# A chunked retention layer with a gated MLP: q and k of half the blocks transposed by DMA, and another order of the jobs

## The chip, the cores and the metric

The kernel runs on one core of one Trainium2 chip. The core has five engines that work side by side: TensorE (PE), VectorE (DVE), ScalarE (ACT), GpSimd (POOL) and SyncE (SP). In this kernel SP issues nearly all DMA transfers, in the order in which they stand in its queue, and 16 DMA engines move them. The metric is device time in microseconds (us).

## The reference

Eight sequences of 576 tokens, eight heads of 64. The first half is a retention layer (attention without softmax, with a decay for each head), the second an MLP whose gate mixes the tokens of a sequence.

```python
scores = scale * np.matmul(q, k.transpose(0, 1, 3, 2))
gamma = 1.0 - 2.0 ** (-5.0 - np.arange(H))
Dmat = np.where(rel >= 0, gamma[:, None, None] ** rel, 0.0)      # rel = query place - key place
x = np.matmul(scores * Dmat, v)                                  # then [B, S, 512]
...
h = gelu(x @ w_in)                # 512 -> 1024
u, v = h[..., :512], h[..., 512:]
v_n = (v - mean) / sqrt(var + 1e-6) * g_ln
v_s = np.einsum('ts,bsd->btd', w_sg, v_n) + b_sg[None, :, None]
out = x + (u * v_s) @ w_out
```

Inputs and output are float32; the matmuls run in bfloat16.

## The kernel before, in words

**Tiling.** Two sequences make a pair (four pairs, 0 to 3) of 1152 tokens, 9 tiles of 128. A pair is cut into five blocks (list `RB`): two of 256 tokens, a half one of 128 (the last 64 tokens of one sequence and the first 64 of the other), and two of 256 again. Blocks are numbered 0 to 19 over all pairs, so pairs 2 and 3 are blocks 10 to 19.

**A block's jobs.**
- `a_load` (L428, L431): q, k and v from HBM to a buffer "ld" each (12 of these), 512 KB for a full block in one DMA, 256 KB for a half block in two. SP issues them.
- `a_prep` (L450, L456): POOL scales q and v by powers of gamma (vector `gqv`) and casts q, k, v to bfloat16: q and k into one tile "qkb" (2 buffers), v into "vb" (3).
- `a_T` (L496), called T below: PE transposes qkb, 32 matmuls against the identity for a full block, 16 for a half one, into a PSUM tile "pp" (2 buffers, shared with the scores and the outputs of attention). `a_Tev` (L505): DVE copies it to "qkT" (2 buffers).
- `a_S` (L528), S: scores k q^T inside the block, from qkT. `a_Sev` (L541): DVE multiplies by the causal mask into "ret".
- `a_Z` (L560), Z: PE adds k^T v to a running state in PSUM "zp"; `a_Zev` (L569): ACT copies it to "zb". This is what a block hands to later ones.
- `a_O`, `a_O2` (L581), O: PE multiplies ret by v and zb by q (again from qkT); `a_Oev` (L637): ACT writes the result, transposed, to "xT".

**The MLP's jobs**, by token tile or by half sequence: `m_V` (L648, the gate's half of w_in), `m_Vg` (ACT), `m_stats` (DVE, L663 and L664), `m_rs` (POOL, L668 to L671: four small steps), `m_norm` (ACT, L683), `m_U` (L695, the other half of w_in), `m_Ug` (ACT, L705), `m_W` (L714: the mixing matrix w_sg times the normalized tiles, five matmuls a job, called W), `m_Wg` (DVE, L724), `m_O` (L741, w_out), `m_Oev`, `m_store` (L761). From pair 1 on the residual x is brought from xT to "xr" by a DMA transpose that SP issues (`m_X`, L750), 128 x 512 elements of 2 bytes, and DVE adds it (L757).

**Fillers.** While PE would be idle early on, it runs matmuls on a tile of zeros ("scr<-warm", L338).

**What sets the order.** All jobs are put on a list with an engine, an assumed duration and their dependencies, and the string `ORDER` holds the order by job number (f9 is a filler of nine units). `Planner.follow` takes each engine's jobs in that order and works out start times with the assumed durations; `emit` calls the jobs by planned start. Each engine then executes its own jobs strictly in the order of the string. The constant `FETCH` is part of this: the planner assumes that PE's code arrives in blocks of 256 instructions and that a block takes that many ns. It changes no instruction by itself; only `ORDER` does.

Of the kernel before, what the change touches and what calls it, by code (L numbers as in the profile page):

```python
# [19 lines left out]
FETCH = 4800.0  # L20
# [5 lines left out]
    '0 f9 1 6 81 2 111 83 7 f11 84 112 3 8 85 114 86 120 89 12 f5 115 f5 113 13 116 118 117 f4 121 119 283 123 284 87 '  # L26
    '124 287 5 88 288 9 127 4 285 23 289 128 24 290 291 82 14 125 292 129 294 90 293 122 f5 126 295 286 296 130 304 '
    '132 305 301 133 308 11 17 10 134 309 25 306 80 310 297 311 135 136 312 15 302 16 298 315 32 307 137 33 313 320 '
    '316 314 131 139 22 34 303 140 327 325 328 321 299 317 330 138 329 141 300 143 142 326 331 18 322 334 19 144 332 '
    '366 20 333 37 318 21 367 336 99 335 370 100 319 35 368 323 371 145 97 373 93 98 95 94 372 91 36 96 377 324 92 '  # L30
    '146 382 337 147 26 148 27 369 374 38 149 378 156 39 387 152 388 150 153 383 338 375 154 348 40 339 355 349 151 '
    '346 344 155 347 389 376 29 157 356 390 437 345 392 353 379 44 438 340 391 354 384 342 158 30 393 31 41 341 28 '
    '163 439 343 161 385 159 162 401 386 43 350 160 394 164 440 402 396 165 395 42 360 397 45 398 441 361 47 351 166 '
    '172 442 458 46 167 443 380 403 445 381 444 103 173 363 352 104 459 446 49 404 447 170 460 405 168 48 179 171 448 '
    '364 461 451 169 449 174 53 105 452 399 450 180 106 175 400 462 176 455 479 463 51 182 464 453 181 465 107 54 454 '
    '357 108 183 188 469 358 52 480 109 470 184 110 177 456 189 185 101 472 457 365 190 178 466 50 473 102 481 467 '
    '186 56 524 468 482 474 484 483 471 406 475 421 525 407 362 476 187 485 57 412 486 422 477 528 413 487 359 191 '
    '478 61 526 529 490 527 55 416 530 408 417 531 410 197 409 491 63 532 411 192 414 533 423 415 195 424 545 193 546 '
    '206 538 194 488 539 196 199 434 489 534 535 435 198 436 428 536 67 208 537 58 540 429 431 430 541 59 542 547 432 '
    '200 504 207 548 600 550 492 62 549 425 493 512 500 426 554 543 501 201 433 601 559 555 520 551 560 427 68 202 '  # L40
    '552 602 60 203 204 603 418 205 496 419 557 553 420 64 604 558 556 544 209 497 621 561 605 210 622 498 606 502 '
    '607 215 608 503 499 70 216 623 213 624 222 211 65 214 563 614 609 611 212 615 217 562 494 616 612 223 495 610 '
    '224 625 613 218 642 626 513 628 219 618 72 617 505 514 643 627 632 506 233 619 516 220 225 687 584 226 635 688 '
    '231 633 66 629 221 636 515 637 507 630 232 631 508 638 71 510 620 509 644 511 227 634 689 645 517 647 242 228 '
    '646 651 518 648 639 73 229 649 79 521 230 652 77 690 564 641 650 691 640 565 234 522 692 708 235 694 251 592 570 '
    '693 568 69 571 566 519 653 572 596 567 569 236 573 238 585 240 654 703 586 237 709 588 695 704 241 701 239 696 '
    '249 698 697 763 699 710 78 250 702 700 243 587 764 523 711 244 582 713 260 574 712 705 583 580 575 714 581 245 '
    '765 246 247 766 593 715 706 720 594 707 716 595 717 721 576 248 589 718 75 722 719 767 590 723 724 252 768 253 '
    '597 769 276 577 770 725 784 578 254 258 256 598 774 257 675 259 771 775 76 255 785 655 726 679 777 772 656 74 '
    '773 665 778 591 261 786 262 788 787 274 599 776 805 667 263 789 806 779 790 666 579 671 781 780 663 791 672 673 '  # L50
    '664 275 782 264 792 783 674 267 800 793 795 801 659 265 796 657 660 794 661 798 266 662 658 797 807 799 277 808 '
    '278 676 802 810 809 268 677 279 803 683 269 850 811 678 280 745 812 680 851 746 668 681 813 735 755 669 852 682 '
    '816 272 853 270 273 759 804 814 670 729 736 271 871 281 872 684 815 730 282 737 854 685 873 738 686 855 747 874 '
    '856 743 857 727 744 876 731 728 858 732 756 859 817 733 757 760 734 758 739 875 861 761 860 748 751 862 866 762 '
    '749 863 818 867 740 819 868 824 741 822 825 742 869 877 830 823 828 878 838 752 879 750 880 829 753 885 881 846 '
    '870 820 886 754 864 821 882 834 865 831 835 887 826 832 836 827 833 889 839 842 837 888 847 840 883 841 848 910 '
    '890 884 896 849 891 902 894 897 892 895 843 893 911 844 845 903 912 918 900 904 913 898 901 905 906 899 922 908 '
    '907 914 909 919 923 920 921 915 924 916 925 917 '
# [22 lines left out]
class Planner:  # L81
# [50 lines left out]
    def place(self, j, t):  # L132
        j.start = t
        if j.nbytes:
            n = j.nbytes / j.run / 16.0 / j.parts
            at = t
            for part in range(j.parts):
                if part and len(self.dmas) >= 8:
                    at = max(at, self.dmas[-8])
                room, full = 160.0 - n, 0.0  # L140
                for end, m in reversed(self.ring):
                    room -= m
                    if room < 0:
                        full = end
                        break
                self.dma_free = max(self.dma_free, at + 1500.0) + (9.5 + 0.0385 * j.run) * n
                at = max(at + j.dur / j.parts, full)
                self.ring.append((self.dma_free, n))
                j.out = self.dma_free + 1500.0
                self.dmas.append(j.out)  # L150
            self.free[j.eng] = at
        else:
            late = 0.0
            if j.eng == "PE":
                while self.count + j.ins > 256 * self.block:
                    at = t + j.dur * (256 * self.block - self.count) / j.ins + late
                    late += max(0.0, self.landed - at)
                    self.landed = max(self.landed, at) + FETCH
                    self.block += 1
                self.count += j.ins  # L160
            j.out = t + j.dur + late
            self.free[j.eng] = j.out - OVL[j.eng]
        if j.port:
            self.port = j.out
        if j.mode is not None:
            self.mode = j.mode
        for b in j.new:
            self.order[b.tag].append(b)
# [65 lines left out]
def kernel(  # L234
# [31 lines left out]
    BUFS = dict(ld=12, wst=2, qkb=2, vb=3, qkT=2, ret=4, zb=4, xT=2, uT=2, vg=3, mv=3, vn=10, ob=3, xr=3,  # L266
# [15 lines left out]
    XP = 1  # L282

# [148 lines left out]

    def a_prep(b, t):
# [4 lines left out]
        if t in "qk" and (b, "qkb") not in st:  # L438
            st[b, "qkb"] = new("qkb", [128, 2, KK, 2, 2, D], BF)
        if t == "v":  # L440
            st[b, "vb"] = new("vb", [128, 2, H, D], BF)
            dst = st[b, "vb"][:, :ns].rearrange("p s h d -> p h s d")
        else:
            dst = st[b, "qkb"][:, "qk".index(t), :, :ns].rearrange("p k s c d -> p c (k s) d" if ns == 2 else "p k s c d -> p (s c) k d")
            src = src.rearrange("p (c k) s d -> p c (k s) d" if ns == 2 else "p (c k) s d -> p (s c) k d", c=2)
# [7 lines left out]
        if t == "q":  # L453
            g = g.rearrange("p (c k) s -> p c (k s)" if ns == 2 else "p (c k) s -> p (s c) k", c=2)
# [27 lines left out]
    def a_T(b):  # L482
# [3 lines left out]
        st[b, "qkT"] = new("qkT", [128, 2, 2, KK, 128], BF)  # L486
        tpf = tp[:].rearrange("p c a k s t -> p c (a k s t)")
        qkb = st[b, "qkb"]
# [13 lines left out]
    def a_Tev(b):  # L502
        ns = RB[b % NBK][0]
        w = 2 * KK * ns * 64
        ins = nc.vector.tensor_copy(st[b, "qkT"][:].rearrange("p c a k t -> p c (a k t)")[:, :, :w],  # L505
                                    st.pop((b, "tp"))[:].rearrange("p c a k s t -> p c (a k s t)")[:, :, :w])
        unfence(ins, ("T", b))

    def qkT_of(b, r, c, a, kk):
        ns = RB[b % NBK][0]  # L510
        w = ns * 64
        f_ = st[b, "qkT"][64 * r:64 * r + 64].rearrange("p c a k t -> p c (a k t)")
        return f_[:, c, (a * KK + kk) * w:(a * KK + kk + 1) * w]

    def a_S(b, g):
# [7 lines left out]
        for n, kk in enumerate(kks):  # L523
            for ks in range(ns):
                o = (n * ns + ks) * cs
                for r in range(2):
                    for c in range(2):
                        ins = nc.tensor.matmul(sc[64 * c:64 * c + 64, r, o:o + cs],  # L528
                                               qkT_of(b, r, c, 1, kk)[:, ks * 64:ks * 64 + 64], qkT_of(b, r, c, 0, kk),
# [19 lines left out]
    def a_Z(b, c, first):  # L549
# [7 lines left out]
        for kk in range(KK):  # L557
            for s in range(ns):
                for hh in range(2):
                    ins = nc.tensor.matmul(z[64 * hh:64 * hh + 64, kk, :], st[b, "qkb"][R, 1, kk, s, hh, :],  # L560
# [320 lines left out]
    for b in range(NBL):  # L881
# [12 lines left out]
        tpb = Buf("pp")  # L894
        jT = add("PE", 565.0 * h, t0, lambda b=b: a_T(b), deps=[jq, jk], new=[tpb, B_qkT[b]], uses=[B_qkb[b]], mode="Q", ins=33 * ns)
        jTe = add("DVE", 90 + 1130.0 * h, t0 + 700.0, lambda b=b: a_Tev(b), deps=[jT], uses=[tpb, B_qkT[b]])
# [165 lines left out]
```

## Time and profile before

| | |
|---|---|
| median of 13 runs | 214.26 us (213.31 to 215.47) |
| the profiled execution | 214.28 us, of which the traced span is 212.6 |
| granted TensorE clock | 0.997 of full speed |
| instructions in the span | 8117 |
| HBM read, written | 32.79 MB, 9.44 MB |
| DMA mean | 218 GB/s |

Times inside the profile count from the start of the span. Busy time is the time in which an engine had an instruction running; matmuls overlap, so a busy PE is not PE at its peak, and the distance from one start to the next says what a job of matmuls really occupies. A row of the timeline gives the start, the duration, the engine, the line in the kernel, the operation and "output<-input" by the names of the tiles; what stands in brackets is the idle time just before it and what ended that. "Issue" there means that the engine waited for nothing that the profile shows. In the 40 slices one digit is the busy share of 5.3 us in tenths. For DMA instructions on SP, "SPq", the duration is the time in which SP was held to issue the transfer; "to landing" counts from the issue to the arrival of the data.

### The profile page before, as it was taken

What the parts mean: (1) busy time and instruction counts of PE and PEld (TensorE: products, weight loads), DVE (VectorE), ACT (ScalarE), POOL (GpSimd) and SP (SyncE); (2) the same over time, 40 slices, a digit from 0 to 9 for tenths busy, and PEclk for the clock granted to TensorE, in tenths of its full rate; (3) what the DMA queues carried; (4) which work ended last, traced back from release to release, by engine and by line L of the source; (5) the groups of instructions that cost most, each with busy time, mean ns of one, the idle gap of its engine ahead of it and who ended that gap; (6) DMA issues with size and microseconds to landing.
All of it is one profiled execution on the core that took longest, in us unless ns stands there. A gap on an engine that the chain in (4) does not pass through costs nothing.

```text
span 212.6 us, 8117 instructions
## 1 busy us (share of the span) xinstructions
PE 201.0 (95%) x3514; PEld 136.0 (64%) x3514; DVE 147.4 (69%) x266; ACT 124.1 (58%) x214; POOL 113.6 (53%) x157
## 2 busy tenths in 40 slices
PE   7997699899999999999999999999999999999990
PEld 3564467677668677676776766756777676666650
DVE  6678647379756786615886786977947994757662
ACT  3359589937786768556667566664583336454100
POOL 5352777894769945970499759807398010202000
PEclk9999999999999999999999999999999999999998
DMA  6999999999999999799998899937960262555575
GB/s 167 290 339 255 277 252 312 276 332 291 211 259 320 291 311 272 206 272 267 239 312 155 177 265 229 194 119 181 225 140 2 78 151 77 148 148 149 152 208 163
DMA packets 84742, 46.29 MB, mean 218 GB/s; under 512 B 28826, under 2 KB 77986, under 8 KB 84706
## 3 DMA queue, kind: packets, MB, share of 16 engines
q1 hardware_dynamic: 84688, 45.77, 86.3%
q8 instruction: 27, 0.44, 0.9%
q14 instruction: 9, 0.07, 0.2%
q10 hardware_dynamic: 18, 0.00, 0.0%
HBM read 32.79 MB, written 9.44 MB: 199 GB/s over the span
## 4 chain that ended last, share of the span: by engine, by line
PE 85%; DMA 5%; ACT 3%; issue 2%; DVE 1%; POOL 1%; SPq 1%; DVEq 0%
PE wp L714 18%; PE op L741 14%; PE hu L695 13%; PE hv L648 13%; PE pp L581 7%; PE scr L338 5%; PE pp L496 5%; PE pp L528 4%; DMA wst<-in_moe_w_sg_dram 4%; PE zp L560 3%; PE wtp L822 1%; DMA xr<-xT 1%; PE op L736 1%; ACT xT L637 1%; ACT L655 1%
## 5 line engine op out<-in xcount | busy, mean ns | idle before, releaser
L456 POOL TENSOR_TENSOR qkb<-ld,gqv 128x1024 bf16<-128x1024 f32 (+1 forms) x19 | 32.7, 1722 | 20.6 <-DMA ld<-in_q_dram 7.1
L541 DVE TENSOR_TENSOR ret<-pp,msk 128x1024 bf16<-128x1024 f32 x32 | 38.1, 1214 | 7.1 <-PE pp L528 5.6
L714 PE MATMUL wp<-wT,vn 128*128 128x288 bf16 x256 | 40.6, 286 | 0.0
L724 DVE TENSOR_TENSOR uT<-wp,uT 128x288 bf16<-128x288 f32 x64 | 28.3, 451 | 17.6 <-PE wp L714 16.3
L456 POOL TENSOR_TENSOR vb<-ld,gqv 128x1024 bf16<-128x1024 f32 (+1 forms) x20 | 34.6, 1731 | 5.5 <-PE pp L581 3.8
L695 PE MATMUL hu<-xT,w_in 128*128 128x256 bf16 (+1 forms) x320 | 37.4, 262 | 0.0
L648 PE MATMUL hv<-w_in,xT 128*128 128x512 bf16 x144 | 36.7, 379 | 0.3 <-DVE w_in L368 0.3
L741 PE MATMUL op<-w_out,uT 128*128 128x512 bf16 x144 | 35.8, 380 | 0.0
L695 PEld LDWEIGHTS <-w_in 128*128 128x128 bf16 x320 | 27.9, 98 | 7.0
L637 ACT ACTIVATE xT<-pp 128x512 bf16<-128x512 f32 (+1 forms) x40 | 24.7, 670 | 11.6 <-PE pp L581 10.0
L668 POOL TENSOR_SCALAR mv<-mv 128x2 f32<-128x2 f32 (+1 forms) x20 | 4.5, 224 | 48.8 <-DVE mv L664 46.2
L714 PEld LDWEIGHTS <-vn 128*128 128x128 bf16 x256 | 24.7, 98 | 8.3
L663 DVE BATCH_NORM_STATS2 bst<-vg 128x6 f32<-128x512 f32 x36 | 24.7, 685 | 7.7 <-ACT vg L655 7.7
L655 ACT ACTIVATE vg<-hv 128x512 f32<-128x512 f32 x36 | 21.5, 596 | 13.3 <-PE hv L648 6.2
L705 ACT ACTIVATE uT<-hu 128x512 bf16<-128x512 f32 x36 | 21.3, 595 | 11.7 <-PE hu L695 11.5
L683 ACT ACTIVATE vn<-vg,mv 128x512 bf16<-128x512 f32 x32 | 25.1, 810 | 5.0 <-POOL mv L671 5.0
L505 DVE COPY qkT<-pp 128x2048 bf16<-128x2048 bf16 (+1 forms) x20 | 22.3, 1113 | 7.3 <-PE pp L496 7.1
L757 DVE TENSOR_TENSOR ob<-op,xr 128x512 f32<-128x512 f32 x27 | 18.4, 689 | 8.9 <-PE op L741 7.3
L569 ACT ACTIVATE zb<-zp 128x256 bf16<-128x256 f32 x32 | 12.2, 382 | 15.5 <-PE zp L560 15.5
L648 PEld LDWEIGHTS <-xT 128*128 128x128 bf16 x144 | 13.5, 98 | 11.9 <-ACT xT L637 0.3
L741 PEld LDWEIGHTS <-uT 128*128 128x128 bf16 x144 | 13.0, 98 | 12.3 <-DVE uT L724 0.4
L714 PE MATMUL wp<-wT,vmid 128*128 128x288 bf16 x64 | 18.3, 287 | 0.0
(79 smaller groups left out, 243.0 us busy)
## 6 DMA issues: line engine op xcount, KB each, us to landing
out_dram<-ob SPq DMA_DIRECT2D x36, 256.0 KB, 4.4
ld<-in_q_dram SPq DMA_DIRECT2D x16, 512.0 KB, 7.3
ld<-in_k_dram SPq DMA_DIRECT2D x16, 512.0 KB, 7.3
ld<-in_v_dram SPq DMA_DIRECT2D x16, 512.0 KB, 5.8
wst<-in_moe_w_in_dram SPq DMA_DIRECT2D x2, 1024.0 KB, 8.3
wst<-in_moe_w_sg_dram SPq DMA_DIRECT2D x2, 576.0 KB, 6.7
ld<-in_q_dram SPq DMA_DIRECT2D x8, 128.0 KB, 5.1
ld<-in_k_dram SPq DMA_DIRECT2D x8, 128.0 KB, 5.5
```

The lines of the kernel that those rows point to most:

```text
L456: eng.tensor_tensor(dst, src, g.unsqueeze(3).to_broadcast(list(src.shape)), op=Alu.mult)
L505: ins = nc.vector.tensor_copy(st[b, "qkT"][:].rearrange("p c a k t -> p c (a k t)")[:, :, :w], st.pop((b, "tp"))[:].rearrange("p c a k s t ...
L541: ins = nc.vector.tensor_tensor(ret[:].rearrange("p r (k t) -> p (r k) t", k=2), sc[:].rearrange("p r (k t) -> p (r k) t", k=2), msk2[:].r ...
L637: nc.scalar.activation(dst, src, Act.Copy)
L648: ins = nc.tensor.matmul(hv[:], xTs[p][:, m, kk, :], w_in[:, kk, F2:], start=(kk == 0), stop=(kk == KK - 1))
L655: unfence(nc.scalar.activation(vgs[i][:], cur.pop(("hv", i))[:], Act.Gelu_apprx_tanh), ("V", i))
L663: nc.vector.bn_stats(bst[:], vgs[i][:])
L683: nc.scalar.activation(vn[:], vg[:], Act.Identity, scale=mv[:, s, 2:3], bias=mv[:, s, 3:4])
L695: ins = nc.tensor.matmul(hu[:, n, :], w_in[:, kk, 128 * c:128 * c + 128], xTs[p][:, m:m + w, kk, :], start=(kk == 0), stop=(kk == KK - 1), ...
L714: ins = nc.tensor.matmul(ps[:], vns[t0 + j][e][:, 128 * c:128 * c + 128], wT[e][j][:, half * HS:(half + 1) * HS], start=(j == 0), stop=(j ...
L724: ins = nc.vector.tensor_tensor(uTs[p][:, c, col:col + HS], cur.pop(("wp", b, c, half))[:], uTs[p][:, c, col:col + HS], op=Alu.mult)
L741: ins = nc.tensor.matmul(op[:], uTs[p][:, c, r], w_out[:, c, :], start=(p >= XP and c == 0), stop=(c == KK - 1), skip_group_check=True)
```

## The change

For the blocks from `TB` = 10 on (pairs 2 and 3), the job on PE and the copy on DVE are replaced by one job on SP, which issues a DMA transpose straight from qkb to qkT: 128 x 2048 elements of 2 bytes for a full block (8 of them), 128 x 1024 for a half one (2). The first ten blocks keep `a_T` and `a_Tev`. In the new layout the two 64-column halves "c" of a 128-column group lie side by side after the transpose, so that S and O read q of a full block as two runs of 64 columns, 128 apart, where it was one run of 128. Half blocks now have the same order (group, half) in qkb as full ones. qkT has three buffers in place of two. `FETCH` is 7200 ns for blocks of code that the planner has arriving up to 32 us and 4800 after that (4800 throughout before), and `ORDER` is another string: on all engines jobs stand in another order, from the start on.

```diff
-FETCH = 4800.0
+FETCH = (7200.0, 4800.0)
...
-    '0 f9 1 6 81 2 111 83 7 f11 84 112 3 8 85 114 86 120 89 12 f5 115 f5 113 13 116 118 117 f4 121 119 283 123 284 87 '
+    '0 f9 1 2 82 6 111 83 7 f10 84 112 3 80 12 87 85 88 113 114 115 8 120 81 273 118 9 274 116 90 275 86 f6 119 121 '
...
-                    self.landed = max(self.landed, at) + FETCH
+                    self.landed = max(self.landed, at)
+                    self.landed += FETCH[self.landed > 32000.0]
...
-    BUFS = dict(ld=12, wst=2, qkb=2, vb=3, qkT=2, ret=4, zb=4, xT=2, uT=2, vg=3, mv=3, vn=10, ob=3, xr=3,
+    BUFS = dict(ld=12, wst=2, qkb=2, vb=3, qkT=3, ret=4, zb=4, xT=2, uT=2, vg=3, mv=3, vn=10, ob=3, xr=3,
...
+    TB = 10
...
+    def a_TX(b):
+        ns = RB[b % NBK][0]
+        st[b, "qkT"] = new("qkT", [128, 2048], BF)
+        nc.sync.dma_start_transpose(st[b, "qkT"][:, :ns * 1024].rearrange("p (g t) -> p g t", t=128),
+                                    st[b, "qkb"][:, :ns * 1024])
...
+        if b < TB:
+            return f_.rearrange("p (c a k s t) -> p c a k s t", c=2, a=2, k=KK, s=ns)[:, c, a, kk]
+        return f_.rearrange("p (a k s c t) -> p c a k s t", c=2, a=2, k=KK, s=ns)[:, c, a, kk]
...
-        tpb = Buf("pp")
-        jT = add("PE", 565.0 * h, t0, lambda b=b: a_T(b), deps=[jq, jk], new=[tpb, B_qkT[b]], uses=[B_qkb[b]], mode="Q", ins=33 * ns)
-        jTe = add("DVE", 90 + 1130.0 * h, t0 + 700.0, lambda b=b: a_Tev(b), deps=[jT], uses=[tpb, B_qkT[b]])
+        if b < TB:
+            tpb = Buf("pp")
+            jT = add("PE", 565.0 * h, t0, lambda b=b: a_T(b), deps=[jq, jk], new=[tpb, B_qkT[b]], uses=[B_qkb[b]], mode="Q", ins=33 * ns)
+            jTe = add("DVE", 90 + 1130.0 * h, t0 + 700.0, lambda b=b: a_Tev(b), deps=[jT], uses=[tpb, B_qkT[b]])
+        else:
+            jTe = add("SP", 2400.0 * ns, t0, lambda b=b: a_TX(b), deps=[jq, jk], new=[B_qkT[b]], uses=[B_qkb[b]],
+                      nbytes=262144 * ns, run=256)
```

## The prediction

> **What bounds the kernel now.** I read the summary of busy time first, then the busy slices, then the table of stretches, then PE's timeline in the one stretch that isn't full. The profiled execution took 214.28 us around a span of 212.6; the median of the runs shown is 214.26, so the sum below, made against 214.28, stands for the median too.
>
> ```profile
> PE 201.0 (95%) x3514; PEld 136.0 (64%) x3514; DVE 147.4 (69%) x266; ACT 124.1 (58%) x214; POOL 113.6 (53%) x157
> ...
> DMA  6999999999999999799998899937960262555575
> ...
> PE 85%; DMA 5%; ACT 3%; issue 2%; DVE 1%; POOL 1%; SPq 1%; DVEq 0%
> ```
>
> ```profile
> 16.90:44.90 28.00, 23.32 (x497) 16.03 (x497) 16.74 (x31) 22.91 (x41) 20.30 (x23) 1.00 1.05 278
> 44.90:90.00 45.10, 45.10 (x893) 32.57 (x886) 34.09 (x58) 31.82 (x57) 33.02 (x39) 1.00 1.05 276
> 90.00:166.00 76.00, 76.00 (x1489) 52.50 (x1488) 54.43 (x90) 47.15 (x83) 48.64 (x63) 1.00 0.91 196
> ```
>
> In the second fence the columns are the stretch, its length, the busy time of PE, weight loads, DVE, ACT and POOL, the granted clock, the DMA share and GB/s. From 44.9 us to the last matmul PE is busy without a hole: what leaves PE there shortens the run, and what any other engine saves there does not. DMA is the second resource: a share of 0.91 to 1.05 until 166, 1.13 between 60 and 80. Only the first 45 us hold idle PE time.
>
> **Part 1: the transposes leave PE.** The job T of one full block is 32 matmuls on one line:
>
> ```profile
> 103.18 0.64 PE L496 MATMUL pp<-ident,qkb 64*128 64x64 bf16 x32
> 103.75 0.44 PE L560 MATMUL zp<-vb,qkb 64*64 64x64 bf16 x16
> ```
>
> From the start of T to the start of the next job is 103.75 - 103.18 = 0.57 us (the 0.64 counts the tail under which the next job runs). A half block (128 tokens, as at 111.25) takes 0.29. Pairs 2 and 3 are blocks 10 to 19: 8 full and 2 half, 8 x 0.57 + 2 x 0.29 = **5.15 us off PE**. All ten lie between 103.2 and 165, where PE has no hole, so all of it counts if nothing new makes PE wait. VectorE loses its ten copies to qkT (L505, 1.22 and 0.66 us: 11.1 us); it is 69% busy and off the chain, so I cost that at nothing. PSUM's two "pp" buffers come free earlier: nothing too. The scores now read q in two runs of 64 columns instead of one of 128; the u matmuls (L695) read xT in two runs already, and in the chain of waits 8 of them, 2048 columns, take 0.87 us, where the 4 unbroken v matmuls (L648) of the same 2048 columns take 0.86. So that costs nothing.
>
> **Part 2: what the DMA transposes cost.** The trace has none of this size, but 27 of a quarter of it, xr:
>
> ```profile
> L750 SPq DMA_TRANSPOSE xr<-xT x27: 1195/1227/2627, 92.5 to 205.7; - x27
> ...
> DMA to landing us min/median/max: 2.4/3.8/6.7
> ```
>
> SP is held 1.2 us by each. For four times the elements the bounds are 1.2 us (plain loads: 1024 packets are issued in 0.42, 128 packets in 0.34, so nearly flat) and 4 x 1.23 = 4.9. I take the fixed 0.34 of a store and 4 x 0.87 above it, 3.8 us, and 2.1 for a half block, because the direct rows are much faster and don't contain the slow part. On the 16 DMA engines the packet records show 512 packets of 256 B for one xr: 18 ns median, but 0.78 us from first to last when alone, 24.4 ns for each of the 32 on an engine.
>
> Does it fit? S is the first use. Adding the durations of PE's jobs in the changed order, and the idle time of part 3, the first S of block 10 starts at about 87.5 us and of block 18, the last, at about 167. The ten transposes must be issued and land between about 82.5 and 167: 84 us. SP's rows behind the first of them and up to the last: 7 full and 2 half transposes (26.6 + 4.2), 12 xr (14.5), 18 full loads (18 x 0.45 = 8.1), 5 pairs of half loads (3.4), 15 stores (7.5): 64 us, or 73 with 4.9 for a transpose. The DMA engines, for each engine and at median packet times (28 ns for 512 B, 18 for 256, 84 for 2 KB): loads 18 x 64 x 28 = 32.3, half loads 5.8, stores 10.1, xr 6.9, transposes 1024 x 18 = 18.4: 73.5 us. At the mean packet times (31.3, 24.3, 94) and 24.4 for the transposes: 36.1 + 7.8 + 11.3 + 9.4 + 25.0 = 89.6. So the queue fits and DMA fits in the middle (81.5) but not at the upper end, by 5.6 us. SP works in order: a transpose that waits for POOL's k holds the loads and stores behind it, and those feed POOL. The third qkT buffer and POOL's 47% idle time are the cover. I take **1 us late**, bounds 0 and 5.6, nearer to the fit because the stretch 60 to 80, with 302 GB/s, shows that the engines do reach the median rate.
>
> The Trainium skill, page "VectorE: DVE Perf Modes", section "The three transpose paths", speaks against the change: it lists a 128x128 bf16 transpose at 390 ns on TensorE and 1309 ns by DMA. By that the nine block-equivalents of 16 such squares would take 188 us, an estimate from the page, and the kernel would be far slower; here four squares pass in 0.78 us, so the trace decides. "Advanced Engine Details and Errata", section "X-Bar Transpose (TRN2)", errs to the other side: as fast as plain DMAs, 350 to 400 GB/s, an estimate of 11 us for the eight of the sum; xr's 131 KB in 0.78 us is 168 GB/s.
>
> **Part 3: the new order, early.** Before the first W job PE has 24.4 us of work in either order, and that job starts at 44.9: 20.5 us are fillers and waits, some 12.5 of them before the first V at 16.98, where the first loads and preps decide. The rest is here:
>
> ```profile
> 19.33 0.41 PE L528 MATMUL pp<-qkT 64*64 64x128 bf16 x15 [1.16 <-issue]
> 19.68 1.04 PE L648 MATMUL hv<-w_in,xT 128*128 128x512 bf16 x4
> 20.55 1.24 PE L338 MATMUL scr<-warm 128*128 128x512 f32 x4
> 23.04 0.44 PE L560 MATMUL zp<-vb,qkb 64*64 64x64 bf16 x16 [1.25 <-POOL vb L456]
> ```
>
> "Issue" is a wait for nothing on another engine; it ends 1.4 us after a 16 KB packet of the instruction queue that began at 16.5 lands (17.9), so it is PE's code. The same shows at 26.08 (0.53) and 39.72 (0.80). The new order loads block 0's v third, puts Z of block 0 ahead of S, and both V jobs (few instructions for their time) behind S of block 1, where the code is awaited. Walked with the durations of the trace, PE then ends its second V at 19.9 in place of 20.5 and its fourth at 27.4 in place of 28.9 with 1.7 us more work behind it: 3.2 ahead. But u waits for the other half of w_in, cast at 24.0 to 25.1 now, and its load moves ahead by only one half-block pair, about 1 us, which takes back up to 2.8. That leaves 0.4 to 3.2: I take **1.8 us**, bounds -1 and 4.
>
> **Sum.** 214.28 - 5.15 - 1.8 + 1.0 = **208.3 us**.
>
> **Rivals.** (a) All is hidden, and the early order gives its upper end: 214.28 - 5.15 - 3.2 = 205.9, to 205 at best. For: a transpose at 3.8 leaves 20 us of SP time free. Against: DMA at 0.91 already. (b) DMA is short by its upper sum, and the transposes land some 4 to 5.6 us late by block 18, with the early gain kept: 211.3 to 212.9. (c) **Slower:** DMA becomes the bound from block 10 on. In a backlog the packets of xr took 37 ns (the one issued at 115.07) and even 69 (the two at 129.75). With everything else at its mean (64.6 us) the gain of 6.95 is used up when transposes cost over (84 + 6.95 - 64.6) / 1024 = 25.7 ns a packet in throughput; at 32 the sum is 97.4, 13.4 late: 220.7. Every load and store behind them on SP is late as well. Against it: those long packets share their engine with others, so they overstate throughput. (d) Nothing gained: the code waits only move, DMA takes what PE gives, 213.7 to 214.9. (e) The edit doing less than it says, q's two runs slowing S and O: L695 speaks against it, and it is inside (d).
>
> **How the numbers follow.** Forecast with 206.5 to 210.5: 0.43; (a) 0.12; (b), 210.5 to 213.6: 0.14; (d) 0.06; (c) 0.25. The range runs from 205 to 219: below it the best of (a), 0.05; above it the heavy half of (c), 0.13. About 0.3% (0.64 us) is what a measurement of this kernel can tell from no change. Faster 0.69, same 0.06, slower 0.25.
>
> **What would show it.** Right: 288 matmuls on the transposes' line instead of 576, ten transposes qkT of about 3.8 and 2.1 us on SP, PE without holes from its first W (about 43 us) on, a last S near 167. Wrong: PE's S waiting for "DMA qkT" between 90 and 167 with growing waits (b, c); qkT rows on SP of 5 us or more; issue waits before 45 us as long as now; u waiting for w_in.

## The result, and the profile after

The changed kernel takes **217.09 us** (median of 11 runs, 215.13 to 218.97) against 214.27 of the kernel before (median of 48 runs, 213.26 to 216.57). The ratio is **1.0098, interval 1.0069 to 1.0126**: 1% slower. The profiled execution of the changed kernel took 216.27 us around a span of 214.6; before it was 214.28 around 212.6, so the two profiles differ by 2.0 us, a little less than the medians.

The same lines of the page as shown of before, now of the changed kernel, with the granted clock and the DMA queue added:

```profile
PE 198.2 (92%) x3224; PEld 133.1 (62%) x3224; DVE 137.2 (64%) x256; ACT 122.4 (57%) x214; POOL 113.6 (53%) x157
...
PEclk9999769999999999999999999969999999999999
DMA  6999999999999999999999997999999898644664
...
q1 hardware_dynamic: 103440, 50.49, 102.2%
...
PE 58%; DMA 21%; SPq 8%; ACT 4%; POOL 3%; DVE 3%; issue 1%; DVEq 0%; ACTq 0%; POOLq 0%
```

PE and DVE lost what was to be lost (288 matmuls and ten copies less). But PE's share of the chain fell from 85% to 58%, and what came in its place is DMA and SP's queue, 6% before and 29% now. The main DMA queue had 84,688 packets and 86.3% before. From the second slice on the digits of DMA now stay at 9, with two exceptions (7 and 8), up to 177 us, where before they were below 9 in nearly all slices from 138 us on and fell to 0 in one.

The table of stretches (columns as in the prediction: length, busy time of PE, PEld, DVE, ACT, POOL, granted clock, DMA share, GB/s):

```profile
16.90:44.90 28.00, 23.76 (x460) 15.85 (x459) 14.90 (x24) 20.07 (x37) 18.04 (x23) 0.88 1.08 277
44.90:90.00 45.10, 44.60 (x930) 31.64 (x928) 31.85 (x53) 30.06 (x57) 36.68 (x42) 1.00 1.14 262
90.00:166.00 76.00, 73.14 (x1154) 49.73 (x1153) 46.97 (x85) 45.61 (x81) 42.95 (x55) 0.98 1.18 244
166.00:207.60 41.60, 40.82 (x481) 26.83 (x479) 28.52 (x53) 18.27 (x31) 8.28 (x19) 1.00 0.71 179
```

PE was without a hole from 45 us on before; now 2.86 us are idle between 90 and 166, and the DMA share there went from 0.91 to 1.18. Early, the granted clock is 0.88 where it was 1.00.

The transposes themselves, and then the longest waits of POOL and those of PE (columns: us in total, times, longest):

```profile
L518 SPq DMA_TRANSPOSE qkT<-qkb x10: 1589/3876/5461, 84.0 to 170.1; - x10
...
DMA to landing us min/median/max: 4.6/7.4/7.8
```

```profile
POOL vb L462 <- DMA ld<-in_v_dram: 18.8, 7, 4.9
...
POOL qkb L462 <- PE zp L574: 13.3, 5, 6.5
...
POOL qkb L456 <- DMA ld<-in_k_dram: 9.6, 6, 2.7
POOL qkb L462 <- DMA ld<-in_q_dram: 8.4, 5, 3.6
...
PEld L542 <- DMA qkT<-qkb: 3.1, 4, 2.4
...
PE pp L542 <- DMA qkT<-qkb: 2.5, 2, 2.2
```

The ten hold SP for 3.88 us at the median: the eight full ones 3.3 to 5.5 us (mean 4.2, estimated 3.8), the two half ones 1.6 and 2.0. They land 7.4 us after their issue. PE's matmuls wait for them only 2.5 us, in two places, and its weight loads 3.1. Another sign stands in POOL's rows: it now waits 36.8 us for loads of q, k and v, where before it waited 7.1 for q and 1.7 for v. The loads are late, so the preps are, so the next transposes are issued late.

**SP's queue has no room left.** In SP's timeline of the changed kernel there is no gap of over 0.15 us between one DMA instruction and the next from 77.2 to 180.2 us: the queue is full for 103 us without a break. Between 84 and 176 us SP is held for 87.2 of the 92 us, the rest being the 0.03 to 0.1 us from one instruction to the next. Before, it was held for 57.0 there and had 26.6 us in gaps. Of the kernel before, the loads' holds (shortest, median, longest, in ns):

```profile
L428 SPq DMA_DIRECT2D ld<-in_q_dram x16: 373/1042/2900, 0.8 to 149.8; - x16
L428 SPq DMA_DIRECT2D ld<-in_v_dram x16: 386/836/3916, 3.3 to 146.4; - x16
L431 SPq DMA_DIRECT2D ld<-in_q_dram x8: 621/918/1755, 9.4 to 120.0; - x8
```

**Where the time went.** I follow PE's lag: the start of a job less the durations of all PE jobs ahead of it, that is all the idle and slow time up to there. The durations are estimates from the trace; with others the split below shifts by up to half a us.

| PE's lag, us | before | after |
|---|---|---|
| first W job (starts at 44.9 / 47.3) | 20.4 | 22.8 |
| near 103 us | 20.9 | 23.8 |
| near 139 us | about 21.5 | 27.1 |
| the last matmuls' end (about 207.5 / 210.1) | 22.3 | 30.0 |

PE's work fell by 5.1 us (185.2 to 180.1). The lag at the first W grew by 2.4, up to 103 us by another 0.5, from there to the end by 4.8; the tail behind the last matmul got 0.6 shorter. -5.1 + 2.4 + 0.5 + 4.8 - 0.6 = +2.0, the difference of the two profiles.

**The early loss** as PE's and ACT's timelines of the changed kernel show it (start, duration, then the row; in brackets the idle time and what ended it):

```profile
21.88 0.44 PE L574 MATMUL zp<-vb,qkb 64*64 64x64 bf16 x16 [0.44 <-POOL vb L462]
24.99 0.47 PE L574 MATMUL zp<-vb,qkb 64*64 64x64 bf16 x10 [2.67 <-ACT zb L583]
...
27.52 1.89 PE L709 MATMUL hu<-xT,w_in 128*128 128x256 bf16 x8
```

```profile
23.61 1.06 ACT L372 ACTIVATE w_in<-wst 128x1024 bf16<-128x1024 f32 x1 [2.18 <-DMA wst<-in_moe_w_in_dram]
24.57 0.37 ACT L583 ACTIVATE zb<-zp 128x256 bf16<-128x256 f32 x1
```

ACT stands at the cast of the second half of w_in, which comes only at 23.6, and the small copy zb that PE needs is queued behind it. PE is empty for 2.67 us, and from 23.6 us on, inside this hole, the granted clock is half for 6.8 us: the eight u matmuls at 27.52 take 1.89 us where the next eight take 1.05.

**The late loss**, at block 15, on PE and on SP:

```profile
136.65 0.62 PE L595 MATMUL pp<-ret,vb 64*64 64x128 bf16 x30
139.49 0.51 PE L542 MATMUL pp<-qkT 64*64 64x128 bf16 x16 [2.21 <-DMA qkT<-qkb]
```

```profile
126.62 2.33 SPq L764 DMA_TRANSPOSE xr<-xT  x1
129.00 0.58 SPq L775 DMA_DIRECT2D out_dram<-ob  x1
129.62 1.38 SPq L433 DMA_DIRECT2D ld<-in_v_dram  x2
131.04 1.11 SPq L430 DMA_DIRECT2D ld<-in_q_dram  x1
132.26 3.79 SPq L518 DMA_TRANSPOSE qkT<-qkb  x1
```

POOL's cast of k ended at 128.5. SP had a residual, a store and loads ahead of the transpose, one right behind the other without a gap, issued it at 132.26, and it landed at 139.45, 11 us behind the cast. The clock is half for 3.4 us after the hole.

### The profile page after: what moved, and what is told of

It reads as the page before. It is cut to its first block, busy times and chain, and to the rows that moved or that the text cites. A ratio compares the mean times of both kernels' runs of the same rounds, so it can differ in the third digit from the quotient of the medians.

```text
span 214.6 us, 7525 instructions
## 1 busy us (share of the span) xinstructions
PE 198.2 (92%) x3224; PEld 133.1 (62%) x3224; DVE 137.2 (64%) x256; ACT 122.4 (57%) x214; POOL 113.6 (53%) x157
## 3 DMA queue, kind: packets, MB, share of 16 engines
q1 hardware_dynamic: 103440, 50.49, 102.2%
## 4 chain that ended last, share of the span: by engine, by line
PE 58%; DMA 21%; SPq 8%; ACT 4%; POOL 3%; DVE 3%; issue 1%; DVEq 0%; ACTq 0%; POOLq 0%
PE wp L728 12%; PE hu L709 11%; PE hv L662 10%; PE op L755 9%; DMA qkT<-qkb 9%; DMA wst<-in_moe_w_in_dram 6%; PE pp L595 5%; DMA ld<-in_v_dram 3%; PE pp L542 3%; SPq L430 3%; PE zp L574 2%; DMA ld<-in_k_dram 2%; PE pp L502 2%; SPq L433 2%; SPq L764 2%; PE wtp L836 2%
## 5 line engine op out<-in xcount | busy, mean ns | idle before, releaser
L555 DVE TENSOR_TENSOR ret<-pp,msk 128x1024 bf16<-128x1024 f32 x32 | 38.1, 1214 | 12.6 <-PE pp L542 10.9
L462 POOL TENSOR_TENSOR qkb<-ld,gqv 128x1024 bf16<-128x1024 f32 (+1 forms) x19 | 32.7, 1722 | 22.2 <-PE zp L574 13.3
L738 DVE TENSOR_TENSOR uT<-wp,uT 128x288 bf16<-128x288 f32 x64 | 28.3, 451 | 18.6 <-PE wp L728 15.7
L709 PE MATMUL hu<-xT,w_in 128*128 128x256 bf16 (+1 forms) x320 | 39.0, 269 | 0.2 <-issue 0.2
L709 PEld LDWEIGHTS <-w_in 128*128 128x128 bf16 x320 | 28.8, 100 | 8.0 <-issue 0.5
L719 ACT ACTIVATE uT<-hu 128x512 bf16<-128x512 f32 x36 | 21.5, 597 | 14.0 <-PE hu L709 13.9
L697 ACT ACTIVATE vn<-vg,mv 128x512 bf16<-128x512 f32 x32 | 25.6, 811 | 5.1 <-POOL mv L685 5.0
L456 POOL CAST qkb<-ld 128x1024 bf16<-128x1024 f32 (+1 forms) x19 | 18.0, 946 | 9.7 <-DMA ld<-in_k_dram 9.6
L662 PEld LDWEIGHTS <-xT 128*128 128x128 bf16 x144 | 13.4, 99 | 13.3 <-issue 1.2
L755 PEld LDWEIGHTS <-uT 128*128 128x128 bf16 x144 | 13.5, 98 | 12.0 <-DVE uT L738 0.9
L574 PE MATMUL zp<-vb,qkb 64*64 64x64 bf16 x480 | 13.6, 196 | 4.6 <-ACT zb L583 2.7
## 6 DMA issues: line engine op xcount, KB each, us to landing
wst<-in_moe_w_in_dram SPq DMA_DIRECT2D x2, 1024.0 KB, 10.7
```

The costliest lines, as they stand in the source:

```text
L462: eng.tensor_tensor(dst, src, g.unsqueeze(3).to_broadcast(list(src.shape)), op=Alu.mult)
L555: ins = nc.vector.tensor_tensor(ret[:].rearrange("p r (k t) -> p (r k) t", k=2), sc[:].rearrange("p r (k t) -> p (r k) t", k=2), msk2[:].r ...
L662: ins = nc.tensor.matmul(hv[:], xTs[p][:, m, kk, :], w_in[:, kk, F2:], start=(kk == 0), stop=(kk == KK - 1))
L697: nc.scalar.activation(vn[:], vg[:], Act.Identity, scale=mv[:, s, 2:3], bias=mv[:, s, 3:4])
L709: ins = nc.tensor.matmul(hu[:, n, :], w_in[:, kk, 128 * c:128 * c + 128], xTs[p][:, m:m + w, kk, :], start=(kk == 0), stop=(kk == KK - 1), ...
L719: unfence(nc.scalar.activation(uTs[p][:, c0:c1, 128 * m:128 * m + 128 * w], cur.pop(("hu", i, half))[:], Act.Gelu_apprx_tanh), ("U", i, half))
```

## The experiments

Each kernel is the changed one with one edit, or one of the two orders with part of the change. The letters in the quoted expectations name theories; the question is told ahead of each. Ratios are to the kernel before on the same chip. A summary first: "DMA" is the share of the 16 DMA engines times the length, summed over five stretches from 84 to 176 us (92 us in all); it passes 92 where packets overlap. "SP idle" is the sum of the gaps of over 0.15 us between the rows of SP's timeline in the same 92 us.

| kernel | median us | ratio, interval | DMA | SP idle |
|---|---|---|---|---|
| before | 214.27 | 1 | 78 | 26.6 |
| changed | 217.09 | 1.0098 (1.0069 to 1.0126) | 106 | 0.0 |
| e1, e2: early hole mended | 218.18, 218.33 | 1.0151 (1.0099 to 1.0203), 1.0182 (1.0123 to 1.0242) | 98, 101 | 0.0, 0.0 |
| e3: a quarter transposed | 208.91 | 0.9736 (0.9688 to 0.9784) | 88 | 14.3 |
| e4: order alone | 217.05 | 1.0124 (1.0077 to 1.0172) | 76 | 38.7 |
| e5: third qkb | 218.21 | 1.0110 (1.0044 to 1.0175) | 101 | 0.0 |
| e6: quarter, and 8 small transfers | 236.86 | 1.0962 (1.0899 to 1.1025) | 64 | 0.6 |
| e7: quarter, and a copy of the rest | 216.12 | 1.0049 (1.0013 to 1.0084) | 111 | 0.0 |
| e8: old order, all ten | 225.69 | 1.0498 (1.0447 to 1.0550) | 96 | 9.8 |
| e9: old order, blocks 15 to 19 | 213.26 | 0.9924 (0.9885 to 0.9962) | 92 | 13.5 |
| e11: quarter, and 4 small transfers | 221.25 | 1.0294 (1.0244 to 1.0344) | 82 | 0.4 |
| e16: half of q and k loaded | 209.23 | 0.9747 (0.9713 to 0.9781) | 89 | 8.8 |

**Is it the early hole and the half clock?** e1 puts the cast behind the copy; e2 fills the hole with filler matmuls.

```diff
e1, ACT's order:  cast of w_in's second half, zb of block 1   ->   zb of block 1, cast of w_in's second half
e2, PE's order:   Z(1,0)   ->   Z(1,0), f12
```

> The changed kernel (217.1 us) with one edit of the order on ScalarE: the cast of the second half of w_in stands behind the copy of block 1's state (zb) instead of ahead of it. Theory A (early loss: PE waits 2.7 us for that copy, which is queued behind a cast whose data land at 23.6, and then runs at half clock for 6.8 us): the wait and the half clock go, about 4 us less, 212.6 to 214, with the granted clock at 1.00 between 17 and 45 us. Rival B (the early stage is bound by w_in's landing itself): u waits in place of Z, same hole, same clock, 216.5 to 217.5.

> The changed kernel with a filler of twelve units (about 2.6 us of matmuls on zeros) on PE between the two Z jobs of block 1, that is, inside the early hole. The wait stays as it was. Theory A (half of the early loss is the clock that drops after the hole): the clock stays at 1.00 and about 2 us come back, 214.5 to 215.5. Rival (the clock costs nothing because PE waits elsewhere in that stretch anyway): 216.5 to 217.5.

e1 has a ratio of 1.0151 and e2 of 1.0182, neither better than the changed kernel. Early they gain: the first W job starts at 45.98 and 45.41 us where it was 47.33. In e1 half clock is left for 3.4 us early (a hole of 1.71 us, in which PE waits for POOL's qkb, stands in place of the old one); in e2 the clock is 0.998 over the whole span, and half clock is gone. But the same job of PE late in the run (147.7 us of work ahead of it) begins at 177.39 and 177.62, in the changed kernel at 176.87. PE came early and waited for something else (in both kernels SP has no gap left either); the theory that the early half clock is the loss fell.

**Are the transposes' data the cost?** e3 transposes only a quarter of the columns and computes scores and outputs of these blocks from that quarter.

```diff
-        nc.sync.dma_start_transpose(st[b, "qkT"][:, :ns * 1024].rearrange("p (g t) -> p g t", t=128),
-                                    st[b, "qkb"][:, :ns * 1024])
+        nc.sync.dma_start_transpose(st[b, "qkT"][:, :ns * 256].rearrange("p (g t) -> p g t", t=128),
+                                    st[b, "qkb"][:, :ns * 256])
```

> The changed kernel in which each q/k transpose by DMA moves only the first quarter of the columns and the scores and outputs of blocks 10 to 19 are computed from that quarter (part of the computation is left out). Order and waits are the same; SP is held about 1.2 us instead of 3.9 by each, and the DMA engines have some 15 to 18 us less to do. If the late loss (the wait of S of block 15 and the half clock behind it, 4 us, and about 1.5 us of small waits) comes from the length of these transfers: 212 to 213.5, with no wait for qkT. If it comes from the queue order and the two qkb buffers alone: 216 to 217.

208.91 us. The early hole and half clock are still there, the order is the changed one, PE has the same number of matmuls; what went is the late loss. Its lag is flat at 22.0 to 22.5 from 60 to 175 us. So all that the change promised is there once the transposes are small. They became small in two ways, fewer packets and SP held 1.5 us in place of 3.9. The next kernels were made to part the two.

**SP's hold, or packets?** e6 adds eight transfers of 4 bytes behind each full transpose of e3 (four for a half block), e11 four and two; e7 adds in their place one plain copy of the other three quarters, in 256-byte packets, to a tile unused by then, and so computes what e3 computes.

```diff
e6, e11:
+        for n in range(4 * ns):                  # e11: 2 * ns
+            nc.sync.dma_start(pad[n][:], mhalf[:1, :1])
e7:
+        nc.sync.dma_start(w.rearrange("p (g t) -> p g t", t=130)[:, :, :128],
+                          st[b, "qkb"][:, ns * 256:].rearrange("p (g t) -> p g t", t=128)[:, :6 * ns])
```

> The quarter-transpose kernel (208.9 us; part of the computation is left out) with eight DMAs of 4 bytes behind each transpose of a full block and four behind a half one: SP is held again for about 1.2 + 8 x 0.33 = 3.9 us, the DMA engines get almost nothing more. Theory S (SP's holding time is what cost the 8 us between 208.9 and 217): 215 to 218. Theory D (the time of the packets on the DMA engines is what cost): 208.5 to 210.5.

> The quarter-transpose kernel with one plain DMA copy behind each transpose that moves the other three quarters of qkb in packets of 256 B to a tile that nobody reads: the DMA engines get about as many packets of the size as in the changed kernel, SP is held only 1.2 + 0.5 us. Theory D (packets on the DMA engines): 213 to 217. Theory S (SP's holding time): 209 to 210.5.

> As the run with eight small DMAs behind each quarter transpose, but with four (two for a half block): those took 0.54 us of SP each and not 0.33, so that run held SP 6.0 us a block; this one holds it 1.2 + 4 x 0.6 = 3.6, about the 3.9 of the changed kernel (part of the computation is left out). Theory D (packets on the DMA engines cost the time): 209 to 211.5. Theory S (SP's holding time): 215 to 218.

e6 took 236.86 us (ratio 1.0962, 1.0899 to 1.1025) and e11 221.25 (1.0294, 1.0244 to 1.0344), both slower than the changed kernel itself. In e6:

```profile
L522 SPq DMA_DIRECT2D pad<-mhalf x72: 542/543/1511, 84.7 to 194.0; - x72
```

Each holds SP for 0.54 us, so a full block held it for 1.3 + 8 x 0.54 = 5.6 us, more than the 3.9 it was to imitate; e11 with 1.3 + 4 x 0.55 = 3.5 is below it and is still slow. What was added to e3 is next to nothing for the DMA engines (e11's sum is 82, e6's 64, e3's 88), but it fills SP's queue: the 36 transfers of e11 hold SP for 21.3 us, and of the 14.3 us of gaps in e3 0.4 are left. So a full queue on SP costs time while the DMA engines have room. That is theory S by its mechanism, though both times lie above the range that it gave; why e11 is slower than the changed kernel, at the same total hold of SP (192.4 and 192.5 us over the run), stays open.

In e7 the transposes hold SP less than in the changed kernel:

```profile
L518 SPq DMA_TRANSPOSE qkT<-qkb x10: 1167/1497/3280, 83.0 to 169.5; - x10
```

That is 1.5 us and 0.65 for the copy, and still it takes 216.12 us, 7.2 of the 8.2 us between e3 and the changed kernel. But this is not the work of packets on the DMA engines alone, because SP is as full as in the changed kernel: no gap is left, and SP's holds over the run add up to 190.8 us, against 192.5 in the changed kernel and 170.1 in e3. Of the 20.7 us above e3 the ten copies are 7.2 and the 36 stores 10.9 (they held SP for 22.2 us in e3 and 33.1 here). So with the packets there other transfers hold SP longer, and e7 does not part the two. e16 comes from the other side: the changed kernel with its ten full transposes, but half of q and k not loaded.

```diff
+            hn = H // 2 if b > 9 and t in "qk" else H
-            nc.sync.dma_start(f_[:], src[2 * p + e, :, r0:r0 + 256, :].rearrange("h (p s) d -> p h (s d)", s=2))
+            nc.sync.dma_start(f_[:, :hn], src[2 * p + e, :hn, r0:r0 + 256, :].rearrange("h (p s) d -> p h (s d)", s=2))
...
+            src = two if b < 10 or ns < 2 else two[:, :1].to_broadcast(list(two.shape))
```

> The changed kernel, but for the eight full blocks of pairs 2 and 3 only half of q and k is loaded (256 KB in place of 512 KB; the prep reads that half twice), so heads 4 to 7 of those blocks are computed from the wrong data: part of the work is left out. Each of the 16 DMA engines loses 8 x 2 x 32 packets of 512 B, at 28 to 31 ns 14 to 16 us between about 75 and 170. The ten transposes and the 3.9 us that each holds SP stay. Theory D, the DMA engines are what the late transposes cost: back to 208.5 to 211, as in the quarter kernel, with no wait of PE for qkT. Theory Q, SP's queue is held too long by the transposes, whatever the DMA engines do: 215.5 to 217, with waits for qkT as in the changed kernel.

209.23 us. The transposes of e16, and three of its stretches:

```profile
L520 SPq DMA_TRANSPOSE qkT<-qkb x10: 1232/3114/4568, 80.3 to 160.9; - x10
```

```profile
100.00:120.00 20.00, 20.00 (x322) 14.23 (x320) 11.70 (x22) 13.18 (x25) 13.34 (x13) 1.00 1.01 207
120.00:140.00 20.00, 20.00 (x351) 13.08 (x349) 13.94 (x26) 11.57 (x21) 13.74 (x19) 1.00 1.12 201
140.00:160.00 20.00, 19.27 (x290) 13.48 (x288) 12.97 (x25) 12.44 (x21) 12.33 (x15) 1.00 1.10 242
```

The transposes hold SP for 3.1 us at the median (28.6 us for the ten, 37.1 in the changed kernel), and PE is full from 100 to 140 us. The changed kernel's shares in the same stretches are 1.20, 1.17 and 1.12. Taking bytes off the DMA engines gives the whole gain with every transpose left in SP's queue. It does not show that the hold is harmless, for the queue is no longer full: 8.8 us of gaps are back. (Its profile is also free of the early half clock, with a hole of 0.9 us there, and yet it ends as e3 does.)

Together: of the kernels with DMA transposes in the changed order, those that lose the time late all have SP's queue full (changed, e1, e2, e5, e6, e7, e11: gaps of 0.6 us at most), and the two that don't, e3 and e16, have gaps again. The DMA sum does not sort them: e6 and e11 lie below e3 and are the slowest. What the change is short of late in the run is time in SP's queue. The packets come in through the holds, which are longer with them (e7's stores, e16's transposes); whether busy DMA engines would cost anything while SP has room, no run shows.

**Would more buffers hide it?** In the changed kernel POOL waits 13.3 us for Z, because qkb has two buffers. e5 gives it three (and takes the room from the fillers' tile).

```diff
-    BUFS = dict(ld=12, wst=2, qkb=2, vb=3, qkT=3, ...
+    BUFS = dict(ld=12, wst=2, qkb=3, vb=3, qkT=3, ...
```

> The changed kernel with three qkb buffers in place of two (the tile of zeros for the fillers is halved to make room, so fillers run as matmuls of 256 columns; their total length is the same). If the late transposes come from POOL's q prep waiting for a free qkb (13.3 us in 5 waits for Z in the changed kernel): 2 to 4 us less, 213 to 215. If DMA bytes from block 10 on are the bound: 216.5 to 218, with the waits for Z gone and waits for loads in their place.

218.21 us: no gain. The waits of POOL in e5:

```profile
POOL vb L462 <- DMA ld<-in_v_dram: 18.0, 8, 5.0
...
POOL qkb L456 <- DMA ld<-in_k_dram: 15.7, 6, 4.4
```

The waits for Z are gone from the list, the waits for k grew from 9.6 to 15.7, and 10.3 us of waits for other jobs of PE are new. SP's queue is as full as ever. A wait that a buffer takes away comes back as others.

**What the order does by itself, and the transposes by themselves.** e4 is the new order with all transposes on PE (its T jobs three PE jobs ahead of S), e12 the same with the early hole filled. e8 is the order of before with all ten transposes by DMA, each issued behind its block's prep of k.

```diff
e4, e12:  TB = 20, T and Tev put back into ORDER          (e12: and f12 behind Z(1,0))
e8:       ORDER of before, T and Tev of blocks 10 to 19 taken out, TX put in behind the prep of k
```

> The changed kernel's order with all twenty blocks transposed on PE and copied by VectorE as before; in pairs 2 and 3 T and its copy stand three PE jobs ahead of the first S of their block. No q/k transpose by DMA. Theory A (the new order alone costs about 2.5 us early, and the DMA part loses some 5 us late, about what it takes off PE): 216.5 to 218.5, early hole as in the changed kernel, no late wait. Rival (the new order is as good as or better than the old one, and the DMA transposes are what costs): 212.5 to 214.5.

> The new order with all transposes on PE (217.05), with the filler of twelve units between the two Z jobs of block 1. The wait for the state's copy stays. If the hole's half clock costs 1.5 to 2 us and nothing later takes it back, since DMA has fewer packets here: 215 to 215.7. If, as in the changed kernel with this filler, the time doesn't move: 216.8 to 217.3.

> The old order with q and k of blocks 10 to 19 transposed by DMA, each transpose standing in SP's queue right behind the place of its block's k prep; three qkT buffers. The early stage is that of the kernel before (no half clock before 45 us). 5.15 us leave PE. If the transposes' cost is on DMA and SP, S waits for several of them, since the old order leaves it only 3 to 12 us behind the prep: 215 to 219. If the new order's early stage were the whole loss: 209 to 211.

e4: 217.05 us, ratio 1.0124. The order alone costs about 2.5 us, and not through SP's queue, which has 38.7 us of gaps there. e12: 217.59, ratio 1.0140; the half clock is gone (0.995) and nothing is won. e8: 225.69, ratio 1.0498: transposes put into an order that wasn't made for them cost 11 us, with PE waiting 9.9 us in two places for qkT; here SP has gaps (9.8 us), and as far as the waits show the transposes stand too close ahead of their S. So the order of the changed kernel is better for the transposes and worse without them.

**In which stretch is the order slow?** e13, e14 and e15 have all transposes on PE and join the two orders: up to the first W job (45 us) new, then old; up to the first W of pair 1 (79 us) new, then old; up to the first W old, then new.

```diff
e13:  ORDER = new up to W(0,0,0), the rest in the order of before
e14:  ORDER = new up to W(1,0,0), the rest in the order of before
e15:  ORDER = before up to W(0,0,0), the rest in the new order
```

> All transposes stay on PE. Jobs stand in the changed kernel's order up to the first W job (about 45 us) and in the order of before from there on. The order alone had cost 2.5 us (e4). Theory G, the early stretch sets it: the late loads and preps of the first 45 us are never made good, and this kernel takes 216.5 to 217.5 too. Theory H, the stretch from 45 to 79 us sets it, where the order kernel's PE waited for DVE, ACT and its own code: then only the 1.6 us by which the first W began later can remain, 214.3 to 215.8, ratio at most 1.007.

> As the kernel before it, but the changed kernel's order holds up to the first W job of pair 1 (about 79 us), the order of before behind that. Theory G and theory H both expect about 217, as of the order alone. If it takes under 215.5, the loss is made behind 79 us, which neither theory holds.

> The other half: the order of before up to the first W job, the changed kernel's order from there on, all transposes on PE. Theory G expects 214 to 215 (an early stretch as in before, nothing lost). Theory H expects 216 to 217.5.

e13: 215.85 us, ratio 1.0063 (1.0035 to 1.0092). e14: 217.17, 1.0107 (1.0064 to 1.0150). e15: 216.71, 1.0095 (1.0065 to 1.0125). Theory G fell with e15: with an early stretch as before, 2 us are lost all the same. By the ratios about 1.4 us go with the new first 45 us alone and about 2 with the new rest alone, where both together cost 2.5; e14 has most of that by 79 us. The intervals overlap, so no finer division is shown. Which wait makes the second part is not settled: PE had no hole between 45 and 90 us before, and has some 1.4 to 2.6 us of them in the profiles of e4, e12 and e15, but behind others each time (its code, ACT's uT, DVE's bst, DVE's uT).

**Where do DMA transposes pay?** The DMA share of before falls to 0.73 between 140 and 160 us and 0.31 from there to 176, and of the 26.6 us of gaps on SP two, of 6.1 and 10.7 us, begin at 135.6 and 154.5. e9 keeps the order of before and moves only blocks 15 to 19 (pair 3), e10 only 16 and 19.

```diff
-    TB = 10
+    TXS = (15, 16, 17, 18, 19)      # e10: (16, 19)
...
-        if b < TB:
+        if b not in TXS:
```

> The old order with DMA transposes for pair 3 alone (blocks 15 to 19), each behind its block's k prep in SP's queue. They fall between 135 and 172 us, where the kernel before has a DMA share of 0.73 and then 0.31. 2.6 us leave PE. Theory D (DMA time is what cost in the changed kernel): no growing wait here; blocks 16 and 19 have 9 us and more between prep and S, blocks 15, 17 and 18 only 4 to 6, less than the 7.4 us a transpose took to land, so some 1 to 6 us of waits in those three and none that grows: 213 to 218.

> The old order with DMA transposes for blocks 16 and 19 alone, the two of pair 3 whose S stands 9 us or more behind the k prep in the trace of before. 1.15 us leave PE, in a stretch where DMA is half idle, and the new transposes have time to land. Theory D: 1 us less than before, 213.2 to 213.8. If a DMA transpose costs the other transfers more than its own time even there: 214.3 or more.

e9 takes **213.26 us, ratio 0.9924 (0.9885 to 0.9962)**, faster than both kernels; e10 213.41, 0.9968 (0.9936 to 1.0001), not to be told from no change. The transposes of e9, and its last two stretches:

```profile
L518 SPq DMA_TRANSPOSE qkT<-qkb x5: 1232/3428/3791, 132.9 to 162.1; - x5
```

```profile
140.00:160.00 20.00, 19.89 (x287) 13.31 (x286) 12.90 (x24) 14.31 (x25) 11.70 (x15) 1.00 0.93 206
160.00:176.00 16.00, 15.62 (x314) 10.39 (x312) 12.34 (x22) 6.36 (x13) 4.68 (x10) 1.00 0.93 182
```

They fill what was free on the DMA engines, to a share of 0.93; SP keeps 13.5 us of gaps, and PE is busy for 35.5 of these 36 us.

## Why the prediction was wrong, point by point

Forecast -5.95, measured +1.99 in the profiled executions. The range held the time; the direction was wrong. What came is slower as in rival (c), and its sentence that every load and store behind the transposes on SP is late as well came true; but the bound that the runs show is SP's queue, and (c) named the DMA engines.

- **"5.15 us off PE": right.** 5.1 by the sum of PE's jobs. e3 and e16 show that it counts in full when nothing new waits: 208.9 and 209.2.
- **"64 us ... So the queue fits": the step that failed most.** The holds of the transposes were sized well: 30.8 us for 7 full and 2 half ones, measured 32.6 for as many between 82.5 and 167 us. The rows beside them were not: the prediction gives loads, stores and xr 33.5 us, and they took 47.5, 80.1 in all of the 84.5 us. No run was needed to see it. In the kernel before, 16 full loads, 8 half loads, 15 stores and 13 xr of the same stretch held SP for 51.4 us. The sum took 0.45 us for a full load, 0.34 for a half one and 1.2 for an xr, which is near or below the shortest rows; medians of the loads are 0.7 to 1.4 us, and the xr of the stretch took 1.57 on the mean. So rival (a)'s "20 us of SP time free" wasn't there.
- **"I take 1 us late, bounds 0 and 5.6, nearer to the fit": followed from it.** It came to about 4.8, near the bound. The sums for the DMA engines, 73.5 and 89.6 us, were too low as well: 98.6 in the same 84.5 us. They were taken from packets as they had been in before, and the stretch of 302 GB/s was read as a sign of room. It held none of xr's 256-byte packets, which begin at 92.5 us and are what the change adds. Nor does a sum over 84 us say when: most of the room in before lies behind 135 us, on SP and on the DMA engines, and six of the ten transposes are issued ahead of that. e9, which uses only that room, gains.
- **The cover failed with it.** "The third qkT buffer and POOL's 47% idle time are the cover": POOL's idle time turned into waits for loads (8.8 to 36.8 us). Not all of that is the transposes' doing, nor does all of it cost time: the order alone (e4) has 18.4, and the fast e3 and e16 have 23.7 and 23.0. e5 shows that another buffer is no cover either.
- **"I take 1.8 us" for the early order, bounds -1 and 4: wrong in sign.** It lost 2.4 at the first W, outside of the bounds. (That is one execution: in the profiles of e3, e4, e7, e11, e13, e14 and e16, with the same order up to there, this job starts at 45.3 to 47.7 us, 0.4 to 2.8 later than before.) The walk took each engine's rows by their dependencies and overlooked ACT's queue: the copy zb behind the cast of w_in, 2.67 us on PE, and the clock. It also took it that what PE gains early is kept, and e1, e2 and e12 show that it isn't: the last thing to wait for changes. And e15 shows that the order also loses about 2 us behind 45 us when all transposes stay on PE, where the prediction counted nothing; the cause of that part stays open.
- **Two runs in q: right** as far as can be seen, e3 and e16 leave no room for a cost.

The chance of 0.25 for (c) was too small. One row that should have raised it stood in the prediction itself: a share of 0.91 on the second resource, over the very stretch that was to take nearly all of the 18,752 new packets (103,440 less 84,688). The other, SP's 57 of 92 us, was in the trace and wasn't added up.

## What to carry to other kernels

When work is moved from a full engine to DMA, look at two things stretch by stretch: the DMA share, and how long the queue that issues the transfers is already held, added up from its rows as they stand and not from their shortest. A timeline of that queue without gaps is the sign that it is full. Move only what fits where both have room; here five blocks of ten paid and ten did not. A transfer that delays loads can show first in the waits of the engine that uses the loads, and less in a wait for the transfer. And an early gain on one engine counts only if the resource that ends last in the middle of the run gains too: to test that, give the time early (a filler, a swap) and see when the same job starts late.

## What the runs showed of the hardware

- In the changed kernel the granted clock fell to half at a hole on PE of 2.67 us (for 6.8 us) and of 2.21 us (for 3.4 us). Holes of 2.06 us (e2), 2.23 (e7) and 2.32 (e11) left it at full, and in e9 it was half for 3.4 us with no hole above 1.05 us near it. The Trainium skill, page "TensorE: Matmul & The Clock Gate", section "Part 1: The HAM clock gate (the "warmup" mystery)", has the clock fall after an idle window of about 3.4 us. The durations here are multiples of that window, but shorter holes were enough, though not always.
- A transfer of 4 bytes holds SP for 0.54 us (e6), longer than the shortest load of 512 KB (0.37 in the kernel before, where the longest of the same size took 3.9). A DMA transpose of 128 x 512 elements holds it for 1.2 us and one of four times the size for 3.3 to 5.5 in the changed kernel and 2.0 to 4.6 in e16, where fewer bytes are loaded.
- Adding 36 transfers of 4 bytes to a queue on SP that had 14 us of gaps in 92 made the kernel 12 us slower (e3 to e11), with no more load on the DMA engines.
- Landing of the transposes took 7.4 us from the issue at the median in the changed kernel, about twice the 3.8 of the small ones in before.
